# Pooling the queries two steps earlier, loading them one step earlier, and halving three long GpSimd operations

## The chip, the core and the metric

The kernel runs on one core of a Trainium2 chip. The metric is the device time of one execution in microseconds. The kernel before took 839.42 us (median of 3 runs, 837.78 to 840.08). The engines named below are TensorE (PE; its weight loads are PEld), VectorE (DVE), ScalarE (ACT), GpSimd (POOL), and SyncE (SP), which issues the DMA transfers.

## What is computed

The input is q, k and v of shape 4 x 8 x 1152 x 64 (batch, heads, sequence, width), in fp32. Neighbouring rows of q are averaged in twos, which leaves 576 queries per head; attention is taken over all 1152 keys; the heads are put side by side (512 columns), and a block follows with a layer norm, two weight matrices and a residual:

```python
q_pool = q.reshape(B, H, S // 2, 2, D).mean(axis=3)
scores = scale * np.matmul(q_pool, k.transpose(0, 1, 3, 2))
scores = scores - np.max(scores, axis=-1, keepdims=True)
attn = np.exp(scores)
attn = attn / (np.sum(attn, axis=-1, keepdims=True) + 1e-09)
x = np.matmul(attn, v)            # then heads side by side: 4 x 576 x 512
xn = (x - mu) / np.sqrt(var + 1e-06) * g_ln
out = x + np.maximum(xn @ w_ch1, 0.0) @ w_ch2     # w_ch1 512 x 2048, w_ch2 2048 x 512
```

## The kernel before, in words

**Pairs and steps.** Two heads of one batch are a pair; there are 16 pairs, p = 0 to 15. A pair's 1152 pooled query rows (576 of each head) are nine blocks of 128, and each block is a step, so there are 144 steps. Step i works on block i % 9 of pair i // 9. Its scores fill a slot of three banks of PSUM (128 x 1152, fp32); there are two slots, for even and odd steps. The function `step(i)` writes out by hand the order of work on every engine: the row maximum of step i on DVE (L384), its exponential on ACT (L398, into the tile `pe`, of which there are two), the scores of step i + 1 on PE (L365, L373), and further work for steps before and after.

**From the exponential to the product with v.** From step 36 on, the exponential is split into a high and a low fp16 part (tile `hl`). ACT makes the high part (L412). In the next step the low part is made: on DVE (L421), or, for the steps with i % 9 of 2, 5 or 8, on GpSimd as a scaling in place (L254, pe) and a subtraction (L419). Both read `pe`, so the exponential two steps later, which writes the same one of the two `pe` tiles, comes after them. SP then issues a transposing DMA of `hl` to `pt` (L424), and PE multiplies `pt` with v four steps after the scores (L467). Before step 36, transposes run on PE and this chain is absent.

**Queries.** `load_q(p)` (L122) loads the queries of pairs p and p + 1, p even, in four transfers of 288 KB, issued by SP; there are two such buffers. `pool_q(p)` (L161) adds neighbouring rows on GpSimd (one instruction, 128 x 1152). `bound(p, "q")` (L174) takes an upper bound of the sums on ACT (L188). `dup_q(p)` (L168) copies the sums beside themselves on GpSimd. `prep_q` then transposes and splits them (L328, L289, L286). For keys the same is done by `prep_k` (L300, L304).

**Where these are placed.** The list at L816 to L850 places each pair's preparation relative to i0 = 9(p - 1), the first step of the pair before it. `at(i, ...)` puts work at the end of step i, `pre(i, ...)` at its beginning. k is loaded at the end of step i0 - 1 and v at the end of i0. For p = 6, 8, 10, 12 and 14, the queries are loaded at the end of step i0 - 8, pooled at the beginning of step i0 - 5 (for p = 6, i0 - 6), bounded two steps after that, and copied at the end of step i0 - 1. For p = 2 and 4 another branch places them, in steps before 36.

**The block behind the attention.** From step 36 on, layer norm and the two matrix products run in between as "units": each step puts one unit on PE (L619 for the first matrix, L651 for the second), whose result goes from one of two PSUM banks through ACT (L632) and DVE (L633) at the beginning of the next step. ACT does these evacuations ahead of that step's exponential. The weights are loaded in steps 0 to 31 and scaled and split by GpSimd (`w_split_a`, `_b`, `_c`; the last is L797); those of the second half are split in steps 40 to 58. When all steps are over, PE alone works through the remaining units.

Every engine takes its instructions in the order in which they are written here, and an instruction that waits holds up all that are behind it on its engine.

Of the kernel before, what the change touches and what calls it, by code (L numbers as in the profile page):

```python
# [14 lines left out]
ALU = mybir.AluOpType  # L15
# [9 lines left out]
def tile_pooled_attention_moe(  # L25
# [18 lines left out]
    nc = tc.nc  # L44
# [4 lines left out]
    C = S // 128  # L49
# [30 lines left out]
    wsl = const.tile([128, 17, 2, 1024], FP16, name="wsl")  # L80
# [74 lines left out]
    def qt_of(p):  # L155
# [2 lines left out]
            st["qt"] = tr_p.tile([128, 2, 2 * C * 64], FP16, tag="qt", name="qt")  # L158
        return st["qt"]

    def pool_q(p, eng, halves=None):  # L161

        a = raws[p, "q"]
        for o, n in ((0, 128),) if halves is None else halves:
            x = a[o:o + n].rearrange("p h c r d -> p (h c) r d")
            eng.tensor_tensor(x[:, :, 0], x[:, :, 0], x[:, :, 1], op=ALU.add)

    def dup_q(p, eng, halves=None):  # L168
        a = raws[p, "q"]
        for o, n in ((0, 128),) if halves is None else halves:  # L170
            x = a[o:o + n].rearrange("p h c r d -> p (h c) r d")
            eng.tensor_copy(x[:, :, 1], x[:, :, 0])

    def bound(p, which, o=0, n=128, junk=None):  # L174
        st = state(p)
# [163 lines left out]
    def on_pe(i):  # L339

        return 0 <= i < HP * C
# [452 lines left out]

    def w_split_c(n):
        x = wsl[:, n + 1].rearrange("p a n -> p (a n)").bitcast(FP32)
        nc.gpsimd.tensor_tensor(wsl[:, n, 1], x, wsl[:, n, 0], op=ALU.subtract)  # L797
        w_done[n // 4] += 1


# [2 lines left out]
    def at(i, fn, *a):  # L803
        todo.setdefault(i, []).append((fn, a))
# [3 lines left out]
    def pre(i, fn, *a):  # L808
        early.setdefault(i, []).append((fn, a))
# [5 lines left out]
    for p in range(1, NP):  # L815
        i0 = (p - 1) * C  # L816
        at(max(i0 - 1, 0), load, p, "k", nc.sync)
        at(i0, load, p, "v", nc.sync)
        at(i0 + 1, bound, p, "k")
        if p % 2 == 0:  # L820
            if on_pe(i0):
                at(i0 - 4, load_q, p, (nc.sync,))
                at(i0 - 1, lambda p=p: calm.appendleft((lambda n: pool_q(p, nc.gpsimd), 0)))
                at(i0, lambda p=p: calm.appendleft((lambda n: dup_q(p, nc.gpsimd), 0)))
            else:
                x = i0 - (6 if p == 6 else 5)
                at(i0 - 8, load_q, p, (nc.sync,))
                pre(x, pool_q, p, nc.gpsimd)
                at(i0 - 1, dup_q, p, nc.gpsimd)
            at(i0 + 2 if on_pe(i0) else x + 2, bound, p, "q")  # L830
        elif p == 1:
            upper = (64, 64)
            pre(0, behind_scales)
            pre(i0 + 1, pool_q, 1, nc.gpsimd, (upper,))
            at(i0 + 1, dup_q, 1, nc.gpsimd, (upper,))
            at(i0 + 2, bound, 1, "q", *upper)
        else:
            at(i0 + 1, same_q, p)
        if not on_pe(p * C):
            at(i0 + 2, bound, p, "v")  # L840
        pre(i0 + 3, scales_reduce, p, 0, 2 if on_pe(p * C) else 3)
        for n in range(2):
            if on_pe(p * C):
                at(i0 + (5, 7)[n], gate)
            at(i0 + (5, 7)[n], take_v, p, n)
        for n, (fn, u) in enumerate(PREPS):
            late = 1 if on_pe(i0) else 0
            pre(i0 + 4 + n + late, lambda fn=fn, p=p, u=u: preps.append((fn, p, u)))

    for m in range(32):  # L850
        i0 = m
# [6 lines left out]
    this = [0]  # L858
# [3 lines left out]
    def w_splits(part):  # L862
        for n in range(4):
            if part < 2:
                calm.extend((fn, 4 * part + n) for fn in (w_split_a, w_split_b, w_split_c))
                continue
            i0 = 22 + 9 * part + 5 * n // 2
            for x, fn in ((0, w_split_a), (1, w_split_b), (2, w_split_c)):
                at(i0 + x, fn, 4 * part + n)
# [276 lines left out]
```

## Time and profile before

| | |
|---|---|
| median of 3 runs | 839.42 us (837.78 to 840.08) |
| the profiled execution | 839.62 us, its span 837.8 us |
| busy shares of the span | PE 97%, DVE 72%, ACT 67%, POOL 42% |
| mean granted TensorE clock | 0.993 |
| chain that ended last | PE 70%, DVE 12%, ACT 9%, DMA 4% |

A span is the time from the first instruction to the last; the profiled execution's own time is 1.8 us longer. A timeline row gives start and duration in us, the engine, the line of the kernel, the operation, what it writes and reads, its shape, how many instructions were merged, and in brackets the idle time of that engine before it with what ended it.

### The profile page before, as it was taken

To read this page: it belongs to the slowest core of one execution; us is meant where nothing else is said; L and a number is where in the kernel's file an instruction comes from. 1 tells how busy PE (TensorE), PEld (TensorE's weight loads), DVE (VectorE), ACT (ScalarE), POOL (GpSimd) and SP (SyncE) were. 2 spreads that over 40 slices of the span, in tenths; PEclk is the share of its full clock that TensorE was granted. 3 is DMA by queue.
4 is the path that set the end of the run, shared out by engine and by line. 5 is a ranking of instruction groups with operands and counts; after the bars stand their busy time and mean duration, and the time that the engine had idled before them with its cause. 6 is when DMAs were issued, how large, how long until landed. Compare 5 with 4: busy or idle time off the path is not lost.

```text
span 837.8 us, 21673 instructions
## 1 busy us (share of the span) xinstructions
PE 809.8 (97%) x9142; PEld 576.7 (69%) x9142; DVE 606.2 (72%) x1167; ACT 558.4 (67%) x810; POOL 351.8 (42%) x343
## 2 busy tenths in 40 slices
PE   7999999987999989999999999999999999999997
PEld 6787878776666666757576766766666767767764
DVE  3598989887888878797887878888787877522221
ACT  3999898976777868787776777677867676311110
POOL 3020334286899982456452553636343432200000
PEclk9999999999999999999999999999999999999999
DMA  6944474125698998899989988996969866401001
GB/s 146 256 164 156 141 210 163 43 60 113 115 181 141 194 172 191 153 185 185 167 147 166 212 167 144 176 196 113 204 125 194 137 126 131 95 2 26 14 1 25
DMA packets 276018, 115.97 MB, mean 138 GB/s; under 512 B 259280, under 2 KB 259280, under 8 KB 275920
## 3 DMA queue, kind: packets, MB, share of 16 engines
q1 hardware_dynamic: 275568, 113.70, 66.0%
q8 instruction: 71, 1.16, 0.6%
q10 hardware_dynamic: 352, 0.88, 0.5%
q14 instruction: 27, 0.22, 0.1%
HBM read 46.14 MB, written 4.72 MB: 61 GB/s over the span
## 4 chain that ended last, share of the span: by engine, by line
PE 70%; DVE 12%; ACT 9%; DMA 4%; issue 3%; POOL 1%; SPq 1%; ACTq 0%; DVEq 0%; POOLq 0%
PE psum L619 21%; PE psum L651 20%; PE psum L467 10%; PE psum L365 8%; ACT pe L398 3%; DVE mx L384 3%; PE psum L373 2%; PE psum L455 2%; DMA kr<-in_k_dram 2%; PE psum L328 2%; PE psum L431 1%; DVE hl L421 1%; ACT pt L437 1%; PE psum L300 1%; DMA stage<-in_moe_w_ch_dram 1%
## 5 line engine op out<-in xcount | busy, mean ns | idle before, releaser
L384 DVE TENSOR_REDUCE mx<-psum 128x1 f32<-128x1152 f32 x144 | 194.3, 1349 | 21.3 <-PE psum L204 6.9
L398 ACT ACTIVATE pe<-psum,nb,sc 128x1152 f32<-128x1152 f32 x144 | 188.6, 1310 | 13.8 <-DVE r L516 5.7
L651 PE MATMUL psum<-wsl,ht 128*128 128x512 f16 x864 | 196.7, 379 | 0.0
L619 PEld LDWEIGHTS <-wsl 128*128 128x128 f16 x1920 | 170.1, 98 | 22.8 <-issue 4.0
L619 PE MATMUL psum<-xn,wsl 128*128 128x256 f16 x1536 | 177.9, 274 | 3.6 <-DVE ht L633 2.8
L651 PEld LDWEIGHTS <-ht 128*128 128x128 f16 x864 | 80.5, 98 | 88.0
L632 ACT ACTIVATE ht<-psum 128x512 f16<-128x512 f32 x72 | 42.9, 596 | 135.4 <-PE psum L619 134.1
L365 PE MATMUL psum<-kt,qt 64*128 64x512 f16 (+1 forms) x960 | 127.4, 380 | 0.7 <-ACT pe L398 0.5
L412 ACT ACTIVATE hl<-pe 128x1152 f16<-128x1152 f32 x108 | 125.6, 1163 | 3.4
L467 PE MATMUL psum<-vt,pt 128*128 128x65 f16 (+1 forms) x3240 | 117.0, 193 | 0.3 <-DMA pt<-hl 0.3
L467 PEld LDWEIGHTS <-pt 128*128 128x128 f16 (+1 forms) x3240 | 108.5, 100 | 3.1 <-DMA pt<-hl 0.4
L421 DVE SCALAR_TENSOR_TENSOR hl<-pe,hl 128x1152 f16<-128x1152 f32 x72 | 109.4, 1519 | 0.0
L633 DVE SCALAR_TENSOR_TENSOR ht<-psum,ht 128x512 f16<-128x512 f32 x72 | 49.6, 689 | 71.6 <-ACT ht L632 71.6
L254 POOL TENSOR_SCALAR pe<-pe 128x1152 f32<-128x1152 f32 x36 | 42.4, 1178 | 140.5 <-ACT hl L412 140.5
L419 POOL TENSOR_TENSOR hl<-pe,hl 128x1152 f16<-128x1152 f32 x36 | 85.5, 2376 | 3.0
L455 PE MATMUL psum<-pt,vt 128*65 128x128 f32 (+1 forms) x720 | 78.9, 265 | 1.9 <-DVE qt L286 1.9
L455 PEld LDWEIGHTS psum<-pt,vt 128*65 128x65 f32 x720 | 73.1, 140 | 2.2 <-DVE qt L286 2.2
L365 PEld LDWEIGHTS <-qt 64*128 64x128 f16 (+1 forms) x960 | 39.6, 96 | 38.7 <-issue 22.1
L373 PEld LDWEIGHTS <-qt 128*128 128x128 f16 (+1 forms) x320 | 17.2, 99 | 62.9 <-issue 62.7
L286 DVE SCALAR_TENSOR_TENSOR qt<-psum,s,qt 128x384 f16<-128x384 f32 x48 | 29.5, 615 | 34.6 <-ACT qt L289 34.3
L260 POOL COPY gate<-gate 128x1 f32<-128x1 f32 x27 | 5.2, 194 | 110.9 <-DVE gate L259 110.9
L665 DVE SCALAR_TENSOR_TENSOR xb<-psum,inv,xb 128x512 f32<-128x512 f32 x32 | 23.8, 745 | 36.9 <-PE psum L651 36.9
(117 smaller groups left out, 1028.4 us busy)
## 6 DMA issues: line engine op xcount, KB each, us to landing
stage<-in_moe_w_ch_dram SPq DMA_DIRECT2D x32, 512.0 KB, 6.0
kr<-in_k_dram SPq DMA_DIRECT2D x16, 576.0 KB, 4.4
qr<-in_q_dram SPq DMA_DIRECT2D x31, 288.0 KB, 6.2
vr<-in_v_dram SPq DMA_DIRECT2D x15, 576.0 KB, 4.8
out_dram<-xb SPq DMA_DIRECT2D x32, 128.0 KB, 2.4
pt<-hl SPq DMA_TRANSPOSE x108, 4.7
kr<-in_k_dram SPq DMA_DIRECT2D x16, 64.0 KB, 4.1
vr<-in_v_dram ACTq DMA_DIRECT2D x1, 576.0 KB, 7.2
```

What stands on the lines that cost most here:

```text
L365: nc.tensor.matmul(out=sp[o:o + w, c0:c0 + 512], lhsT=qt[r:r + 64, qa, q0:q0 + w], rhs=kt[r:r + 64, ka, h], start=(a == 0), stop=(a == 2),)
L384: nc.vector.tensor_reduce(mx, st["s"], axis=AX.X, op=ALU.max)
L398: nc.scalar.activation(out=st["pe"], in_=st["s"], func=ACTF.Exp, scale=pair[i // C]["sc"][:, 0:1], bias=st["nb"],)
L412: nc.scalar.activation(out=hl[:, 0], in_=st["pe"], func=ACTF.Copy, scale=2.0 ** 15)
L419: nc.gpsimd.tensor_tensor(hl[:, 1], st["pe"], hl[:, 0], op=ALU.subtract)
L421: nc.vector.scalar_tensor_tensor(hl[:, 1], st["pe"], 2.0 ** 15, hl[:, 0], op0=ALU.mult, op1=ALU.subtract)
L455: nc.tensor.matmul(out=ps[0:65, q0:q0 + w], lhsT=vt[:, h, c], rhs=pt[:, 128 * u + q0:128 * u + q0 + w], start=(u == 0), stop=(u == C - 1),)
L467: nc.tensor.matmul(out=dst[:, 0:n], lhsT=lhsT, rhs=rhs, start=(u == 0 and lhsT is hi and n == 65), stop=(u == C - 1 and lhsT is lo), skip_ ...
L619: nc.tensor.matmul(out=ps[:, o:o + n], lhsT=wsl[:, 8 * w + cc, wa, f * 128:f * 128 + 128], rhs=xn[:, xa * KD + cc, 0:n], start=(m == 0), s ...
L632: lambda: nc.scalar.activation(out=hi, in_=pv, func=ACTF.Relu),
L633: lambda: nc.vector.scalar_tensor_tensor(lo, pv, 0.0, hi, op0=ALU.max, op1=ALU.subtract),
L651: nc.tensor.matmul(out=ps, lhsT=hv[0][:, ha, f, t * 128:t * 128 + 128], rhs=wsl[:, 8 * w + 4 + f // 2, wa, (f % 2) * DM:(f % 2) * DM + DM] ...
```

## The change

Three things change. In steps from 36 on, `pool_q`, `dup_q` and `w_split_c` issue two instructions, each for half of the columns, in place of one (`on_pe(i)` is true for steps 0 to 35; `this[0]` is the step being written). For p = 6, 8, 10, 12 and 14 the queries are loaded at the end of step i0 - 9 (was i0 - 8). For p = 8, 10, 12 and 14 they are pooled at the beginning of step i0 - 7 (was i0 - 5; p = 6 keeps i0 - 6), and for all five the bound follows one step after the pooling (was two).

```diff
+    def cuts(x):
+        return (x,) if on_pe(this[0]) else (x[:, 0:C], x[:, C:2 * C])
+
     def pool_q(p, eng, halves=None):
 
         a = raws[p, "q"]
         for o, n in ((0, 128),) if halves is None else halves:
             x = a[o:o + n].rearrange("p h c r d -> p (h c) r d")
-            eng.tensor_tensor(x[:, :, 0], x[:, :, 0], x[:, :, 1], op=ALU.add)
+            for y in cuts(x):
+                eng.tensor_tensor(y[:, :, 0], y[:, :, 0], y[:, :, 1], op=ALU.add)
 
     def dup_q(p, eng, halves=None):
...
-            eng.tensor_copy(x[:, :, 1], x[:, :, 0])
+            for y in cuts(x):
+                eng.tensor_copy(y[:, :, 1], y[:, :, 0])
...
     def w_split_c(n):
         x = wsl[:, n + 1].rearrange("p a n -> p (a n)").bitcast(FP32)
-        nc.gpsimd.tensor_tensor(wsl[:, n, 1], x, wsl[:, n, 0], op=ALU.subtract)
+        for y in (slice(0, 1024),) if on_pe(this[0]) else (slice(0, 512), slice(512, 1024)):
+            nc.gpsimd.tensor_tensor(wsl[:, n, 1, y], x[:, y], wsl[:, n, 0, y], op=ALU.subtract)
         w_done[n // 4] += 1
...
             else:
-                x = i0 - (6 if p == 6 else 5)
-                at(i0 - 8, load_q, p, (nc.sync,))
+                x = i0 - (6 if p == 6 else 7)
+                at(i0 - 9, load_q, p, (nc.sync,))
                 pre(x, pool_q, p, nc.gpsimd)
                 at(i0 - 1, dup_q, p, nc.gpsimd)
-            at(i0 + 2 if on_pe(i0) else x + 2, bound, p, "q")
+            at(i0 + 2 if on_pe(i0) else x + 1, bound, p, "q")
```

## Rows read from the trace of the kernel before

**Rows 1.** The page, part 1: busy us, share of the span, instructions.

```profile
PE 809.8 (97%) x9142; PEld 576.7 (69%) x9142; DVE 606.2 (72%) x1167; ACT 558.4 (67%) x810; POOL 351.8 (42%) x343
```

**Rows 2.** PE's waits from 215 to 730 us: total us, times, longest.

```profile
PE psum L619 <- DVE ht L633: 2.8, 2, 2.1
```

**Rows 3.** PE's timeline, one stretch for each of p = 8, 10, 12, 14.

```profile
303.74 4.34 PE L619 MATMUL psum<-xn,wsl 128*128 128x256 f16 x24 [2.14 <-DVE ht L633]
...
388.02 2.78 PE L619 MATMUL psum<-xn,wsl 128*128 128x256 f16 x24
...
477.59 2.75 PE L651 MATMUL psum<-wsl,ht 128*128 128x512 f16 x12
...
566.26 0.63 PE L574 MATMUL psum<-ident,xs 128*128 128x128 f32 x4 [1.77 <-DVE kt L286]
```

**Rows 4.** Windows: us, busy PE, PEld, DVE, ACT, POOL, granted PE clock, DMA share, GB/s.

```profile
303.70:308.10 4.40, 4.36 (x26) 3.23 (x25) 3.75 (x6) 2.43 (x3) 4.21 (x4) 0.63 0.69 132
```

**Rows 5.** DVE's timeline, the scales of pair 7.

```profile
298.79 1.84 DVE L240 TENSOR_SCALAR e<-red 128x3 int32<-128x3 int32 x1
```

**Rows 6.** SP's timeline: loads of v and q for p = 8, 10, 12.

```profile
285.01 0.58 SPq L119 DMA_DIRECT2D vr<-in_v_dram  x1
...
289.54 2.50 SPq L131 DMA_DIRECT2D qr<-in_q_dram  x4
...
370.84 0.58 SPq L119 DMA_DIRECT2D vr<-in_v_dram  x1
...
375.83 2.50 SPq L131 DMA_DIRECT2D qr<-in_q_dram  x4
...
457.88 0.58 SPq L119 DMA_DIRECT2D vr<-in_v_dram  x1
...
464.08 3.01 SPq L131 DMA_DIRECT2D qr<-in_q_dram  x4
```

**Rows 7.** GpSimd's timeline around the pooling for p = 8, 10, 12.

```profile
285.70 2.13 POOL L797 TENSOR_TENSOR wsl<-wsl 128x1024 f16<-128x1024 f32 x1
287.81 2.22 POOL L254 TENSOR_SCALAR wsl<-wsl,wscl 128x1024 f32<-128x1024 f32 x1
...
291.23 2.38 POOL L419 TENSOR_TENSOR hl<-pe,hl 128x1152 f16<-128x1152 f32 x1
...
297.98 2.62 POOL L166 TENSOR_TENSOR qr<-qr 128x1152 f32<-128x1152 f32 x1 [3.36 <-DMA qr<-in_q_dram]
...
375.92 1.16 POOL L254 TENSOR_SCALAR pe<-pe 128x1152 f32<-128x1152 f32 x1 [6.82 <-ACT hl L412]
...
384.58 2.62 POOL L166 TENSOR_TENSOR qr<-qr 128x1152 f32<-128x1152 f32 x1 [3.10 <-DMA qr<-in_q_dram]
...
473.31 2.62 POOL L166 TENSOR_TENSOR qr<-qr 128x1152 f32<-128x1152 f32 x1 [4.91 <-DMA qr<-in_q_dram]
```

**Rows 8.** ACT's timeline: exponentials of steps 40, 58, 76, 94, and two more.

```profile
210.89 1.31 ACT L398 ACTIVATE pe<-psum,nb,sc 128x1152 f32<-128x1152 f32 x1 [0.79 <-POOL hl L419]
...
289.44 1.16 ACT L188 ACTIVATE kt<-vr 128x1152 f16<-128x1152 f32 x1 [0.42 <-DMA vr<-in_v_dram]
...
295.08 1.31 ACT L398 ACTIVATE pe<-psum,nb,sc 128x1152 f32<-128x1152 f32 x1
...
380.75 1.31 ACT L398 ACTIVATE pe<-psum,nb,sc 128x1152 f32<-128x1152 f32 x1
...
383.48 0.69 ACT L289 ACTIVATE kt<-psum,s 128x512 f16<-128x512 f32 x1
...
471.23 1.31 ACT L398 ACTIVATE pe<-psum,nb,sc 128x1152 f32<-128x1152 f32 x1
```

**Rows 9.** The page, part 5: the evacuations of the first matrix's units.

```profile
L632 ACT ACTIVATE ht<-psum 128x512 f16<-128x512 f32 x72 | 42.9, 596 | 135.4 <-PE psum L619 134.1
...
L633 DVE SCALAR_TENSOR_TENSOR ht<-psum,ht 128x512 f16<-128x512 f32 x72 | 49.6, 689 | 71.6 <-ACT ht L632 71.6
```

**Rows 10.** The line of the copy of the sums: duration in ns, min/median/max.

```profile
L172 POOL COPY qr<-qr x9: 1142/1150/2323, 8.7 to 583.3; 128x1152 f32<-128x1152 f32 x7, 64x1152 f32<-64x1152 f32 x2
```

## The prediction

> **What bounds the kernel now.** I read the busy shares first, then who PE waited for, then the stretches around each pooling, engine by engine. The reader is to see that PE is busy for 97% of the span [rows 1]: what PE loses is lost for good, and what another engine loses costs nothing until PE waits for it. From 215 to 730 us, where the edits lie, PE waits little; the largest entry is 2.8 us in two waits of the first matrix's units (L619) for DVE [rows 2]. Of these, 2.14 us stand at 303.74, in the step of pair 7's scales [rows 3]. Their cause is on GpSimd. A DVE instruction on 128 x 3 numbers takes 1.84 us at 298.79 [rows 5], and ends just after GpSimd's pooling, which runs from 297.98 to 300.60 [rows 7]. After that wait the 24 matmuls take 4.34 us, where the same 24 take 2.78 at 388.02 [rows 3]: the granted clock is 0.63 in that stretch [rows 4], half speed for part of it. So an idle PE costs about 1.6 us more, at least where it stood for 2.1 us; at 566.26 a wait of 1.77 us was followed by no such slowing. These collisions are what the edits take away: 2.14 + 1.56 us at pair 8, and at most 1.77 at pair 14 [rows 3].
>
> **What moves on SP.** The four transfers of q go out one step sooner, directly behind the v transfer of the same step end: at 285.6 instead of 289.54 (285.01 + 0.58), at 371.4 instead of 375.83, at 458.5 instead of 464.08 [rows 6]. That is 3.9 to 5.6 us sooner. They also pass one transposing DMA, which now waits behind them (2.5 to 3.0 us of issuing). Its product with v comes four steps after the scores, and PE will be held by something later in the same steps (below), so I cost it at nothing; without that cover it would be up to 3 us a pair.
>
> **When the data is there.** Before, GpSimd stood 3.36, 3.10 and 4.91 us at the pooling until the data had landed, 8.44, 8.75 and 9.23 us after the first issue (297.98 - 289.54, and so on) [rows 6, 7]. That cost nothing: nothing urgent was behind it. Now v's 576 KB are directly ahead in the same queue; for pair 8 v landed 4.4 us after its issue (289.44 - 285.01) [rows 6, 8]. This adds between 0 and 4.4 us to q. I take 1.0, near the lower end, because v has landed 3.8 us after q's new issue, a time in which most of q was not there before either. The pooling can then begin at 285.6 + 9.4 = 295.0, 371.4 + 9.8 = 381.2 and 458.5 + 10.2 = 468.7.
>
> **What stands behind it.** The pooling moves two steps up GpSimd's queue and the data only one. It now stands in front of the low part of step i0 - 7 (56, 74, 92), which before ran at 290.0 to 293.6 (pair 8), and from 375.92 (pair 10) [rows 7]. GpSimd works in order, so this low part starts only after the data has landed and the pooling is done. Pooling: 2.62 us and 0.13 for a second instruction (bounds 0 and 0.19, for an instruction boundary; other extra instructions on GpSimd, some 20, come to 3 us over the whole run and lie in its idle time). Low part: 1.16 + 0.08 + 2.38 = 3.62. Pair 8 also has the halved split (2.13 + 0.13) and a scaling of weights (2.22, lower bound 1.1) in front [rows 7]. So the low parts end:
> pair 8: 295.0 + 2.75 + 2.26 + 2.22 + 3.62 = 305.9;
> pair 10: 381.2 + 2.75 + 3.62 = 387.5;
> pair 12: 468.7 + 6.37 = 475.1.
> The exponentials of steps 58, 76 and 94 write the same `pe` tile and began at 295.08, 380.75 and 471.23 [rows 8]. They become 10.8, 6.8 and 3.9 us late. That this wait is real is shown once already: at 210.89, where the pooling of pair 6 stands before step 38's low part in the same manner, ACT waited 0.79 us for GpSimd [rows 8]. The bound on ACT, one step earlier after the pooling, waits too (about 1.16 us of work, as at 289.44), but less long than the exponential behind it.
>
> **What PE loses.** Behind the late exponential come ACT's other work, then the evacuations that PE's next unit needs: 2.73 us from the exponential's start to the first evacuation (383.48 - 380.75) [rows 8], then 0.60 on ACT and 0.69 on DVE [rows 9], so 4.0 in all; at pair 10 a key block's 0.69 goes first, so 4.7. PE's unit moves
> at pair 8 from 303.74 to 305.9 + 4.0 = 309.9: +6.2;
> at pair 10 from 388.02 to 387.5 + 4.7 = 392.2: +4.2;
> at pair 12 from 477.59 to 475.1 + 4.0 = 479.1: +1.5 [rows 3].
> Pair 8's old wait and its slowing are inside the 303.74 and stay. Pair 14 lies as pair 12 does, but PE there already waits 1.77 us before 566.26; I put it between 0 and 1.5, at 0.7. Pair 10 would add one stretch at half clock, as at 303.74: +1.6. Pair 6 keeps its place and gets its data sooner; its 0.79 us go, but no wait of PE hangs on it in the rows: 0. Halves of `dup_q` and `w_split_c`: 0, beside work.
>
> Sum: 6.2 + 4.2 + 1.6 + 1.5 + 0.7 = +14.2. The profiled execution took 839.62, so 853.8; it lies 0.2 above the median of the runs, so 853.6 against 839.42.
>
> **A rule beside the rows.** GpSimd's copy of the sums takes 1.15 us in the median and 2.32 at most [rows 10]: GpSimd, too, is held up by something. The Trainium skill, SBUF — State Buffer, section "Who interferes with whom", says that a DVE instruction with two SBUF inputs and a reading GpSimd instruction exclude each other for a whole instruction, and that whichever came first keeps the other out. By that rule the second half of a pooling can lose its turn to DVE's low part, which speaks against halving: 1.17 us (2.32 - 1.15) in front of each of four late low parts, 4.7 us more in all, 858, which is inside the range below.
>
> **Rivals.** (A) The other side, faster: the data lands while GpSimd is idle, the pooling is over before its low part is due, and the collisions are gone. Gain: 2.14 + 1.56 + 1.77 = 5.5, so 834. It decides at pair 10: the pooling must be done by 375.92, so the data must be there by 373.2, 1.8 us after the issue. For it: GpSimd stood idle for 6.82 us before 375.92, just the room for a pooling [rows 7]. Against it: every load needed 8.4 us or more.
> The skill's rule from above stands behind this rival too: a DVE instruction shut out by a half waits half as long.
> (B) Only pair 8 pays, since PE's two score slots and its units swallow the 4 to 7 us at the others: 6.2, so 846. For it: ACT is busy for only 67% [rows 1]; against it: the first matrix's units wait for the evacuation of the same step.
> (C) Every pair pays the whole: v ahead costs the full 4.4 us, and each wait brings a slow clock. 3.4 x 4 + 1.6 x 2 = 17 more, so 871; with half of these 17 us, 862.
> (D) GpSimd's delay stays off PE's path: 839.6. Against it: the wait at 210.89.
>
> **How the numbers follow.** About 0.3% (2.5 us) is what can be told from no change. Chances: forecast 0.54 (its own range 847 to 860: without v's 1.0, the slow clock and half of the 2.22, it is 14.2 - 3.7 - 1.6 - 1.1 = 7.8, so 847; with two more microseconds of landing at three pairs, 860), A 0.11, B 0.17, C 0.12, D 0.06. Slower 0.54 + 0.17 + 0.12 = 0.83, same 0.06, faster 0.11. A range of 842 to 865 leaves out A, D and the uppermost part of C, 0.20 together.
>
> **What would show it.** GpSimd's two poolings for p = 10 start near 381, with a wait for DMA of 8 us or more ahead of them, and step 74's low part follows them, not before 384. ACT waits for GpSimd at the exponentials of steps 58, 76 and 94, which the rows of before show without a wait; PE shows gaps of 2 to 6 us there, some followed by a lower granted clock, and the scales of pair 7 run at 0.2 us each. The prediction is wrong if the poolings begin without a wait, or if PE has no gap after a late low part.

## The result and the profile after

The changed kernel takes 852.42 us (median of 4 runs, 850.33 to 854.45); the kernel before took 838.84 us beside it (4 runs, 837.78 to 840.08). The ratio is 1.015 [1.0121, 1.0179]: 13.6 us slower. The forecast was 853.6, in a range of 842 to 865. The profiled execution after is the slowest of the four, 854.45 us, span 852.6.

The first row below is the page's busy shares after, to hold against [rows 1].

```profile
PE 815.6 (96%) x9142; PEld 580.3 (68%) x9142; DVE 604.8 (71%) x1167; ACT 558.1 (65%) x810; POOL 358.2 (42%) x363
```

The span grew by 14.8 us. PE stood idle for 837.8 - 809.8 = 28.0 us before and 852.6 - 815.6 = 37.0 after: 9.0 of the 14.8. The other 5.8 are PE being busy longer on the same 9142 instructions. What it waited for, from 215 to 745 us (total, times, longest), to hold against [rows 2]:

```profile
PE psum L472 <- DMA pt<-hl: 8.9, 4, 4.3
PE psum L579 <- DVE kt L291: 4.3, 2, 2.4
...
PE psum L624 <- DVE ht L638: 0.9, 2, 0.6
```

The first entry was next to nothing before (L467, 0.3 us in one wait): the product with v (L472, L467 before) waits for the transposing DMA. `kt` had one wait before, of 1.77 us [rows 3]. The timeline of PE shows where:

```profile
301.07 1.65 PE L472 MATMUL psum<-vt,pt 128*128 128x65 f16 x27 [4.28 <-DMA pt<-hl]
...
303.18 4.82 PE L624 MATMUL psum<-xn,wsl 128*128 128x256 f16 x24
...
310.87 2.78 PE L624 MATMUL psum<-xn,wsl 128*128 128x256 f16 x24
...
390.69 0.99 PE L472 MATMUL psum<-vt,pt 128*128 128x65 f16 x27 [3.19 <-DMA pt<-hl]
...
397.03 0.63 PE L579 MATMUL psum<-ident,xs 128*128 128x128 f32 x4 [1.83 <-DVE kt L291]
...
483.05 0.99 PE L472 MATMUL psum<-vt,pt 128*128 128x65 f16 x27 [0.89 <-DMA pt<-hl]
...
572.30 0.99 PE L472 MATMUL psum<-vt,pt 128*128 128x65 f16 x27 [0.53 <-DMA pt<-hl]
...
579.75 0.63 PE L579 MATMUL psum<-ident,xs 128*128 128x128 f32 x4 [2.44 <-DVE kt L291]
```

Each of the four moved poolings has its wait for `pt`; the two with a wait of 3 us or more are pairs 8 and 10. At pairs 10 and 14 a second wait follows, for a key block (`kt`) that DVE evacuates late. After the 4.28 us the next 24 matmuls take 4.82 us, and not the 2.78 they take at full clock [rows 3]. They are the unit that ran at 296.58 before, though. The unit that waited 2.14 us for `ht` at 303.74 [rows 3] is now the one at 310.87: 7.1 us later, without a wait, and at full clock.

The result of each unit is evacuated by ACT and DVE; DVE's part, for these two units of pair 8:

```profile
300.68 0.69 DVE L638 SCALAR_TENSOR_TENSOR ht<-psum,ht 128x512 f16<-128x512 f32 x1 [4.41 <-ACT ht L637]
...
310.12 0.69 DVE L638 SCALAR_TENSOR_TENSOR ht<-psum,ht 128x512 f16<-128x512 f32 x1 [1.85 <-ACT ht L637]
```

They end at 301.37 and 310.81. ACT's part of the first stands behind the bound of 298.90, that of the second behind the exponential of 306.89 (both below). The first is 0.3 us behind the landing of `pt`, the second 0.06 us ahead of its unit: at pair 8 the late evacuations come at the same time as the late DMA.

Where the transposing DMA stands is on SP's queue. After, in two places:

```profile
286.58 0.58 SPq L119 DMA_DIRECT2D vr<-in_v_dram  x1
287.20 2.41 SPq L131 DMA_DIRECT2D qr<-in_q_dram  x4
...
376.95 0.58 SPq L119 DMA_DIRECT2D vr<-in_v_dram  x1
377.57 2.44 SPq L131 DMA_DIRECT2D qr<-in_q_dram  x4
380.18 7.00 SPq L429 DMA_TRANSPOSE pt<-hl  x1
```

and before, the one that stood between v and q:

```profile
371.58 4.20 SPq L424 DMA_TRANSPOSE pt<-hl  x1
```

Before, this transposing DMA was issued 0.7 us after v and took 4.20 us to issue. After, it is issued 3.2 us after v (380.18 - 376.95), has four transfers of q ahead of it as well, and takes 7.00 us. From its issue to its landing it took 6.3 us before and 10.5 after; at pair 8 5.9 before (285.75) and 11.2 after.

GpSimd after, the poolings (two halves, L170) and the low parts (L424) behind them, for p = 8, 10 and 14, to hold against [rows 7]:

```profile
296.12 2.75 POOL L170 TENSOR_TENSOR qr<-qr 128x576 f32<-128x576 f32 x2 [9.68 <-DMA qr<-in_q_dram]
...
304.49 2.37 POOL L424 TENSOR_TENSOR hl<-pe,hl 128x1152 f16<-128x1152 f32 x1
...
386.45 2.75 POOL L170 TENSOR_TENSOR qr<-qr 128x576 f32<-128x576 f32 x2 [11.75 <-DMA qr<-in_q_dram]
...
390.40 2.38 POOL L424 TENSOR_TENSOR hl<-pe,hl 128x1152 f16<-128x1152 f32 x1
...
568.15 1.41 POOL L170 TENSOR_TENSOR qr<-qr 128x576 f32<-128x576 f32 x1 [11.74 <-DMA qr<-in_q_dram]
570.52 1.40 POOL L170 TENSOR_TENSOR qr<-qr 128x576 f32<-128x576 f32 x1 [0.97 <-DVE r L522]
```

ACT after, the bounds (L193) and the exponentials (L403) of steps 58 and 76, to hold against [rows 8]:

```profile
298.90 1.16 ACT L193 ACTIVATE qr<-qr 128x1152 f32<-128x1152 f32 x1 [3.03 <-POOL qr L170]
...
306.89 1.31 ACT L403 ACTIVATE pe<-psum,nb,sc 128x1152 f32<-128x1152 f32 x1 [6.25 <-POOL hl L424]
...
389.23 1.16 ACT L193 ACTIVATE qr<-qr 128x1152 f32<-128x1152 f32 x1 [3.14 <-POOL qr L170]
...
392.81 1.31 ACT L403 ACTIVATE pe<-psum,nb,sc 128x1152 f32<-128x1152 f32 x1 [1.84 <-POOL hl L424]
```

The exponential of step 58 starts 0.03 us after its low part has ended (304.49 + 2.37 = 306.86), that of 76 likewise. These waits were forecast, and they are there.

The longer busy time of PE is its clock. Three stretches, after (us; busy us of PE, PEld, DVE, ACT, POOL with instructions; granted PE clock; DMA share; GB/s):

```profile
186.00:206.00 20.00, 15.81 (x115) 11.88 (x114) 13.61 (x25) 12.80 (x17) 17.25 (x18) 0.83 0.70 138
296.00:312.00 16.00, 11.13 (x111) 8.26 (x108) 9.56 (x16) 6.78 (x10) 15.53 (x14) 0.79 0.80 116
574.00:590.00 16.00, 13.28 (x150) 8.74 (x149) 11.64 (x24) 10.40 (x14) 9.29 (x14) 0.89 0.69 133
```

the same stretches before:

```profile
186.00:206.00 20.00, 14.84 (x122) 10.99 (x123) 13.98 (x29) 13.81 (x19) 13.41 (x13) 0.91 0.62 139
296.00:312.00 16.00, 13.86 (x147) 9.83 (x144) 14.30 (x23) 9.46 (x14) 13.47 (x10) 0.89 0.87 159
574.00:590.00 16.00, 16.00 (x210) 11.64 (x209) 12.89 (x20) 12.18 (x18) 13.67 (x10) 1.00 0.70 123
```

Time lost at half speed is the stretch times what its clock lacks to 1.00: (0.17 - 0.09) x 20 = 1.6 us more than before in the first, 0.10 x 16 = 1.6 in the second, 0.11 x 16 = 1.8 in the third, 5.0 together, most of the 5.8. The second stretch has the wait of 4.28 us, the third that of 2.44. The first lies ahead of the four moved poolings; the run with the pooling behind the low part (below), whose order is the same up to step 56, was granted 1.00 there, so I count it as scatter of this one execution, which is 2.0 us above its median. That leaves 3.4 us beside the waits of this change. And a wait does not always bring a slow clock: at pair 10, with waits of 3.19 and 1.83 us, the clock was full,

```profile
380.00:404.00 24.00, 17.41 (x233) 13.27 (x232) 17.44 (x35) 15.81 (x23) 10.94 (x14) 1.00 0.97 189
```

### The profile page after: what moved, and what is told of

The parts are those of the page before. It is cut to its first block, busy times and chain, and to the rows that moved or that the text cites. A ratio compares the mean times of both kernels' runs of the same rounds, so it can differ in the third digit from the quotient of the medians.

```text
span 852.6 us, 21686 instructions
## 1 busy us (share of the span) xinstructions
PE 815.6 (96%) x9142; PEld 580.3 (68%) x9142; DVE 604.8 (71%) x1167; ACT 558.1 (65%) x810; POOL 358.2 (42%) x363
## 4 chain that ended last, share of the span: by engine, by line
PE 62%; POOL 11%; DVE 9%; ACT 9%; DMA 4%; issue 3%; SPq 1%; POOLq 0%; ACTq 0%; DVEq 0%
PE psum L656 19%; PE psum L624 17%; PE psum L472 9%; PE psum L370 7%; ACT pe L403 3%; DVE mx L389 3%; PE psum L460 3%; POOL wsl L259 3%; POOL hl L424 3%; PE psum L378 2%; POOL wsl L803 2%; DMA qr<-in_q_dram 2%; PE psum L436 2%; PE psum L333 1%; POOL pe L259 1%
## 5 line engine op out<-in xcount | busy, mean ns | idle before, releaser
L403 ACT ACTIVATE pe<-psum,nb,sc 128x1152 f32<-128x1152 f32 x144 | 188.5, 1309 | 25.9 <-POOL hl L424 14.9
L472 PE MATMUL psum<-vt,pt 128*128 128x65 f16 (+1 forms) x3240 | 118.4, 194 | 8.9 <-DMA pt<-hl 8.9
L472 PEld LDWEIGHTS <-pt 128*128 128x128 f16 (+1 forms) x3240 | 109.8, 101 | 12.2 <-DMA pt<-hl 9.6
L424 POOL TENSOR_TENSOR hl<-pe,hl 128x1152 f16<-128x1152 f32 x36 | 85.5, 2374 | 3.0
```

The costliest lines, as they stand in the source:

```text
L403: nc.scalar.activation(out=st["pe"], in_=st["s"], func=ACTF.Exp, scale=pair[i // C]["sc"][:, 0:1], bias=st["nb"],)
L424: nc.gpsimd.tensor_tensor(hl[:, 1], st["pe"], hl[:, 0], op=ALU.subtract)
L472: nc.tensor.matmul(out=dst[:, 0:n], lhsT=lhsT, rhs=rhs, start=(u == 0 and lhsT is hi and n == 65), stop=(u == C - 1 and lhsT is lo), skip_ ...
```

## The experiments

Two theories were set against each other. **W**, that of the prediction: GpSimd stands at the pooling until q has landed, the low part behind it is late, and with it the exponential. **Q**: the transfers of q, issued directly behind v, hold up the transposing DMA behind both, and PE waits for `pt`. The table gives, for the profiled executions, the start of the row maximum at some steps, less that of the kernel before; a jump between two columns is what the pooling in between costs (p = 6 before 54, then p = 8, 10, 12, 14). The first column is scatter of the start. The jump for p = 6 lies between -1.3 and +3.1 among the versions with a sooner load, and is not read here.

| kernel | 36 | 54 | 72 | 90 | 108 | 126 | end | median us | ratio |
|---|---|---|---|---|---|---|---|---|---|
| changed kernel | -0.8 | +0.7 | +5.6 | +10.5 | +11.7 | +14.8 | +14.8 | 852.42 | 1.015 [1.0121, 1.0179] |
| loads alone | +1.1 | +4.2 | +6.3 | +12.5 | +13.1 | +11.6 | +11.6 | 850.53 | 1.0129 [1.0099, 1.0159] |
| poolings alone | +0.9 | +2.3 | +12.9 | +22.2 | +29.1 | +34.4 | +34.4 | 869.54 | 1.0366 [1.0326, 1.0407] |
| halves alone | -1.5 | -0.9 | -3.3 | -1.8 | -1.9 | -3.0 | -3.0 | 836.39 | 0.9967 [0.9951, 0.9983] |
| both moves, no halves | -1.2 | +1.0 | +6.5 | +11.2 | +12.8 | +15.4 | +15.4 | 856.23 | 1.0203 [1.0161, 1.0244] |
| load two steps sooner still | -1.2 | +0.4 | +0.4 | +2.6 | +2.6 | +0.4 | +0.4 | 839.56 | 1.0015 [1.0000, 1.0030] |
| pooling behind the low part | -2.0 | -3.3 | -1.1 | +3.3 | +4.2 | +2.9 | +2.9 | 845.43 | 1.0101 [1.0072, 1.0129] |
| pooling late, halves | -1.9 | -1.6 | -4.1 | -3.2 | -3.2 | -4.2 | -4.2 | 835.92 | 0.9973 [0.9958, 0.9987] |
| half of q sooner | -1.9 | +1.2 | +0.8 | +2.0 | +2.0 | +3.5 | +3.5 | 839.56 | 1.0014 [0.9997, 1.0032] |
| poolings alone, bound later | -0.9 | -0.9 | +6.5 | +13.6 | +20.5 | +28.4 | +28.4 | 870.02 | 1.0393 [1.0346, 1.0439] |
| changed kernel, bound later | -0.1 | -0.7 | +5.5 | +11.6 | +16.5 | +22.3 | +22.3 | 857.23 | 1.0237 [1.0199, 1.0275] |

The kernel before took 838.84 us beside the changed kernel, 839.36 beside the next four rows (loads, poolings, halves, both moves), 838.24 beside the four after them and 837.66 beside the last two. A difference between rows with different neighbours is therefore uncertain by about 1 us.

**Loads alone.** Kernel before, with

```diff
-                at(i0 - 8, load_q, p, (nc.sync,))
+                at(i0 - 9, load_q, p, (nc.sync,))
```

> The kernel before with one edit: the queries are loaded at the end of step i0 - 9 instead of i0 - 8. Theory W (the loss comes from GpSimd, which stands at the pooling and holds the low part behind it): the pooling keeps its late place, its data comes a step sooner, so nothing is lost: 837 to 839 us. Rival Q (the loss comes from the queue: q directly behind v delays the transposing DMA behind both, and the product with v waits for it): the product waits for pt as in the changed kernel, where these waits sum to 8.9 us at four places, so 846 to 850 us, with the pooling itself on time.

850.53 us, 11.2 slower, with the poolings where they always were. PE's waits:

```profile
PE psum L467 <- DMA pt<-hl: 8.0, 4, 3.6
```

As many waits, at the same line, as in the changed kernel, and hardly any other; GpSimd waited 1.0 us for q in all. So Q is real, and alone it costs nearly as much as the whole change (11.2 of the 16.9 us that both moves cost with whole operations, below).

**Poolings alone.** Kernel before, with

```diff
-                x = i0 - (6 if p == 6 else 5)
+                x = i0 - (6 if p == 6 else 7)
...
-            at(i0 + 2 if on_pe(i0) else x + 2, bound, p, "q")
+            at(i0 + 2 if on_pe(i0) else x + 1, bound, p, "q")
```

> The kernel before with one edit: the queries are pooled at i0 - 7 (bound one step behind), the load stays at i0 - 8. Theory W: the data now lands some 4 us later than in the changed kernel while the low part waits behind it, so the exponentials are 4 us later still at each of four pairs: 860 to 872 us, slower than the changed kernel. Rival Q: v and q are a step apart again, so the products with v do not wait: 838 to 843 us.

869.54 us, 30.2 slower. PE does not wait for `pt`; it waits for what comes behind a late ACT, among the entries:

```profile
PE psum L619 <- DVE ht L633: 12.4, 3, 7.3
PE psum L300 <- DVE ht L633: 8.3, 2, 5.1
PE psum L365 <- ACT pe L398: 7.3, 3, 5.6
```

and GpSimd stood up to 20.1 us at a pooling:

```profile
POOL qr L166 <- DMA qr<-in_q_dram: 71.3, 5, 20.1
```

So W is real too. GpSimd stands longer here than in the changed kernel (71.3 us at its poolings, against 47.8 at the four moved ones there), since the data comes a step later; so 30 is not W's price in the changed kernel. Each theory is enough by itself for a slower kernel. Their prices, 11 and 30, don't add: in the changed kernel the late evacuations and the late DMA reach PE in the same microseconds (pair 8 above), and each hides part of the other.

**Halves alone.** Kernel before, with `cuts` and the three split operations of the change, and nothing moved.

> The kernel before with the halved instructions alone. If DVE waits for whole GpSimd instructions, as the 1.84 us on 128 x 3 numbers suggests, the wait of PE at the scales of pair 7 (2.1 us and a slow clock behind it) shrinks by about half and the clock need not fall: 836 to 838 us. If the halves only add instruction boundaries, or lose their turn to DVE: 839 to 841 us.

836.39 us: 0.33% faster, 3.0 us, clear of 1. At pair 8 PE shows why:

```profile
301.77 2.78 PE L624 MATMUL psum<-xn,wsl 128*128 128x256 f16 x24 [0.25 <-DVE ht L638]
```

Here it waited 2.14 us before, and the same 24 matmuls took 4.34 [rows 3]: 1.89 + 1.56 = 3.45 us gone. DVE's instruction in front of it is shorter:

```profile
298.28 1.11 DVE L245 TENSOR_SCALAR e<-red 128x3 int32<-128x3 int32 x1
```

where it was 1.84 [rows 5]. It now ends at 299.39, when the first half of the pooling that began at 297.96 (two halves in 2.75) is over.

**Both moves, no halves.** The changed kernel without `cuts`.

> The changed kernel without the halves (both moves, whole instructions). Theories W and Q both say that the moves make the loss, so 851 to 855 us, like the changed kernel's 852.4. If the halves have a part in it by losing their turn to DVE, this one is faster by up to 4 us: 848.

856.23 us, 3.8 above the changed kernel's 852.42; the intervals of the two ratios overlap, so this alone shows no difference, but the sign is that of the run before. So the two moves cost some 17 us, and the halves give some 3 back.

**Load two steps sooner still.** Changed kernel, with

```diff
-                at(i0 - 9, load_q, p, (nc.sync,))
+                at(i0 - (9 if p == 6 else 11), load_q, p, (nc.sync,))
```

> The changed kernel with one edit: for p = 8 to 14 the queries are loaded two steps sooner still (end of step i0 - 11), away from v's load and three steps before the pooling at i0 - 7. W and Q (each alone is enough for most of the loss) both go: GpSimd finds its data, and no transposing DMA stands behind v and q together. 833 to 838 us, as the halves alone or somewhat faster. If pooling at i0 - 7 costs by itself (GpSimd's time in front of the low part, DVE shut out): 840 to 845.

839.56 us. Both waits are gone, from GpSimd's poolings (but for 1.66 us at p = 12) and from PE's product with v, and 12 to 13 us with them. It missed both of its ranges. One reason in the rows is that k is now late. k's issue before:

```profile
365.24 0.57 SPq L115 DMA_DIRECT2D kr<-in_k_dram  x1
```

and SP, ACT and PE in this run:

```profile
364.02 4.44 SPq L429 DMA_TRANSPOSE pt<-hl  x1
368.56 0.52 SPq L115 DMA_DIRECT2D kr<-in_k_dram  x1
...
373.74 1.16 ACT L193 ACTIVATE kt<-kr 128x1152 f16<-128x1152 f32 x1 [1.58 <-DMA kr<-in_k_dram]
...
376.73 0.84 PE L370 MATMUL psum<-kt,qt 64*64 64x512 f16 x12 [2.15 <-ACT pe L403]
```

On SP q's four transfers (from 360.03), two output transfers and a transposing DMA stand ahead of k. It goes out 3.3 us later than before, of which 0.4 is this run's own lag (column 72), and is there 5.2 us after its issue, 4.3 before. ACT's bound on it stands in front of the exponential, and PE waits 2.15 us for that; at pair 8 it is 1.52. So what is delayed behind q need not be the transposing DMA. But not everything behind q pays: the one at 364.02 comes much closer behind q than k, landed 8.1 us after its issue, and PE did not wait for it. In the kernel before, too, one stands behind q (379.77, 7.4 us to landing) without a wait.

**Pooling behind the low part.** Changed kernel, the load as there, for p of 8 and more

```diff
-                pre(x, pool_q, p, nc.gpsimd)
+                (pre if p == 6 else at)(x + (0 if p == 6 else 1), pool_q, p, nc.gpsimd)
...
-            at(i0 + 2 if on_pe(i0) else x + 1, bound, p, "q")
+            at(i0 + 2 if on_pe(i0) else x + (1 if p == 6 else 2), bound, p, "q")
```

> The changed kernel with one edit: for p = 8 to 14 the pooling is issued behind the low part of step i0 - 7 (end of step i0 - 6, bound one step later), so that GpSimd's wait for the data holds up no low part. The load stays directly behind v. If W has its share in the changed kernel's loss beside Q: 846 to 849 us, the load alone (850.5) less the halves' 3. If Q covers W fully: 852. If W were the whole of it: 836.

845.43 us: 7.0 under the changed kernel (6.4 with each against the kernel before beside it; four runs, 842.55 to 849.45), and a little under the 846 to 849 of the theory that W has its share. The waits for `pt` stay, those for `kt` (L579) are gone:

```profile
PE psum L472 <- DMA pt<-hl: 7.7, 4, 3.5
```

So W's share on top of Q is 6 to 7 us. What is left, 845.43 against halves alone at 836.39, is Q: 9.0, or 10.2 with each against the kernel before beside it. That is close to the 11.2 of the load alone.

**Pooling late, halves.** Changed kernel with the load back at i0 - 8 and, for p of 8 and more, the pooling at i0 - 4.

> A kernel meant to beat both: the halves, the load where it was (i0 - 8; p = 6 as well), and for p = 8 to 14 the pooling one step later than before (i0 - 4), behind the scales of the pair before, bound one step behind it. If the collision of the pooling with the scales of step i0 - 5 is what the halves leave over: 834 to 836 us, against 836.4 for the halves alone. If the pooling there delays taking v and the low part of step i0 - 4: 838 to 842.

835.92 us, 0.27% faster than before and no different from halves alone. PE's largest entry here is 1.7 us, and its wait for `pt` is

```profile
PE psum L472 <- DMA pt<-hl: 0.5, 2, 0.3
```

This and halves alone are the two versions that beat both kernels.

**Half of q sooner.** Kernel before, two of the four transfers at i0 - 9, directly behind v, and two where all were:

```diff
-                at(i0 - 8, load_q, p, (nc.sync,))
+                at(i0 - 9, load_q, p, (nc.sync,), (0,))
+                at(i0 - 8, load_q, p, (nc.sync,), (1,))
```

> The kernel before with the load in two parts: pair p's half of q at the end of step i0 - 9, directly behind v, pair p + 1's half at the end of i0 - 8. Pooling where it was. Theory Q as a matter of bytes ahead of the transposing DMA: with 576 KB instead of 1152 KB behind v, the transposing DMA lands some 4 us sooner than with the whole load, and the product with v waits little: 838 to 842 us. If it is the place directly behind v whatever the bytes: 847 to 851, as the whole load one step sooner (850.5).

839.56 us, no change that can be told, and

```profile
PE psum L467 <- DMA pt<-hl: 2.1, 2, 1.1
```

against 8.0 with all four ahead. The wait hangs on how much is queued in front of the transposing DMA. The one behind v and half of q (374.39) landed 9.1 us after its issue, between the 6.3 behind v alone and the 10.5 behind v and all of q. Fewer bytes and fewer transfers to issue go together here; the run does not part them.

**Which part of W.** ACT has two instructions that wait for a late GpSimd: the bound, for the pooling, and the exponential, for the low part. In two more kernels the bound of pairs 8 to 14 comes one step later, in poolings alone and in the changed kernel:

```diff
-            at(i0 + 2 if on_pe(i0) else x + 1, bound, p, "q")
+            at(i0 + 2 if on_pe(i0) else x + (1 if p == 6 else 2), bound, p, "q")
```

> The kernel before with the poolings of pairs 8 to 14 two steps earlier, their bound on ACT two steps after the pooling (one step in the pooling-only run, 869.5 us), the loads where they were. If the late low part and its exponential hold PE (my prediction's chain), the bound does not matter: 866 to 872 us, ACT's waits for GpSimd's low part at 15 us or more. If it is the bound, which stands on ACT ahead of the evacuations of the same step and waits for the pooling, most goes: 845 to 858, and the wait of 7.3 us of the first matrix's units for DVE's evacuation is gone or below 3 us.

> The changed kernel with the bound of pairs 8 to 14 two steps after the pooling (was one). If the late exponential is what is left of GpSimd's hold beside the transposing DMA: 850 to 854 us, as the changed kernel (852.4), with PE's waits of 1.8 and 2.4 us for the key blocks still there. If the bound carries it: 844 to 848, as the kernel with the pooling behind the low part (845.4). In both, PE's waits for pt stay at 7.5 to 9 us, since the loads are where they were.

The first took 870.02 us (1.0393 [1.0346, 1.0439]), as poolings alone took 869.54: the bound is not what holds PE. The wait for `ht` is down to 2.9 us in all, as the other theory wanted, but others took its place:

```profile
PE psum L574 <- DVE kt L286: 8.3, 1, 8.3
PE psum L365 <- ACT pe L398: 7.5, 3, 4.8
PE psum L574 <- POOL xs L568: 7.0, 1, 7.0
```

The last is a carrier that the prediction did not have: the layer norm's scaling (`xs`) stands on GpSimd behind the same low part. The second kernel took 857.23 us (1.0237 [1.0199, 1.0275]), slower than the changed kernel and outside both expectations. Its waits for `pt` are 8.6 us; the key blocks' grew from 4.3 to

```profile
PE psum L579 <- DVE kt L291: 7.3, 2, 5.0
```

In its rows the bound now runs between the late exponential and the key block's evacuation, 1.15 us in front of it; that this alone makes the 4.8 us is argued, not shown.

## Why the prediction was right, and where it was not

**The total** came out within 1.2 us, and the mechanism it rested on is there. The closeness is in part luck. By pairs the terms were +6.2, +5.8, +1.5 and +0.7, and the table has +4.9, +4.9, +1.2 and +3.1: three too large, one too small. The path to them has one failed step, and several terms were mis-sized.

**Data and low parts: right.** The poolings were put at 295.0, 381.2 and 468.7; they began at 296.12, 386.45 and 478.61. The second is 380.8 and the third 468.1 on the clock of before, since by then the kernel ran 5.6 and 10.5 late (columns 72 and 90). Waits for DMA of 9.68, 11.75, 14.64 and 11.74 us stand ahead of the four. The low parts were to end at 305.9, 387.5 and 475.1: they ended at 306.86 and, less 5.6 and 10.5, at 387.2 and 474.4. The exponentials of steps 58, 76 and 94 wait for GpSimd. The 1.0 us for v ahead of q was 0.1 to 0.5: q was there 8.9, 8.9 and 9.5 us after its first issue (296.12 - 287.20, and so on), against 8.4, 8.8 and 9.2 before.

**From the exponential to PE, at pair 8: right.** The unit of 303.74 was forecast for 309.9; it began at 310.87, and its evacuation ended at 310.81, 3.9 us behind the start of the late exponential (forecast 4.0). The term is smaller than forecast because the old slow clock did not stay: the unit takes 2.78 us and not 4.34. With the 0.7 of column 54, 7.1 - 0.7 - 1.56 = 4.9.

**The failed step: "so I cost it at nothing".** That was the transposing DMA which q's transfers pass on SP, with "without that cover it would be up to 3 us a pair" beside it. The cover was to be the late evacuation behind the exponential. But the product with v stands ahead of the unit, and at all four pairs PE met the DMA first: 8.9 us in all, 4.28 at pair 8, against 4.3 in waits for `kt`, which answer to W. The cover was not wrong altogether: at pair 8 the late evacuations were there no sooner than the DMA, so either cause would by itself have held PE about as long. That is read from the rows; no run has W alone with the data as soon as in the changed kernel. What the runs show is that a kernel that cures only W keeps half of the loss (845.43), that Q alone costs 11.2 us, and that with both cured 1.3 of the 13.6 is left (839.56). The bound of 3 us a pair was too low as well, because it counted only the time to issue q, 2.5 to 3.0. The transposing DMA itself took longer too: 7.00 us to issue behind v and q, 4.20 behind v alone, and 10.5 to landing against 6.3. The Trainium skill, DMA: Bandwidth & Descriptors, section "Queues, rings and completion order", says that a DMA engine takes the descriptors of one ring in order, and that SP owns one ring on each; the runs agree: 8.0 us of waits with all of q ahead, 2.1 with half of it.

**Pair 10: the slow clock (+1.6) did not come.** The clock was 1.00 there (window above). The 4.9 us are the waits of 3.19 and 1.83.

**Halves: 0 was wrong by 3 us.** The prediction named the collision (2.14 us and 1.56 of clock at pair 8) and then let it stay inside the new schedule. Halves alone gave 3.0, and with whole operations the changed kernel took 3.8 us more. Part of the reasoning held: DVE is still caught at pair 7's scales in the changed kernel, not by a pooling but by the low part that has moved there,

```profile
305.02 1.87 DVE L245 TENSOR_SCALAR e<-red 128x3 int32<-128x3 int32 x1
```

which ends at 306.89, as GpSimd's row of 304.49 ends at 306.86. So "the scales of pair 7 at 0.2 us each" failed. The opposite worry, that a second half loses its turn to DVE, shows once in the four poolings, 0.97 us at 570.52, which the profile puts down to DVE's small instructions and not to its low part; I had priced it at 1.17 for each. In the Trainium skill's rule (SBUF — State Buffer, "Who interferes with whom") the loser waits for the end of the winner's instruction; the 1.84 that became 1.11 when the instruction was cut agrees.

**Pair 14: +0.7 was too little.** It cost 3.1: its wait of 1.77 us for a key block [rows 3] became 2.44, the new one for `pt` adds 0.53, and now a stretch at half clock follows (granted 0.89 in the window above, 1.8 us), which after the 1.77 did not.

**Rivals.** A needed q within 1.8 us of its issue; it was there after 8.9. B (846) and C (862 to 871) are outside the measured interval, though C's picture, that every pooling pays fully, is close to poolings alone.

**What stays open.** How the 13.6 us divide between W and Q has no single answer: taking W away gives 6 to 7, and what then remains above halves alone is 9 to 10. When a slow clock follows a wait of PE is open too: it followed waits of 2.14 (before), 2.44 and 4.28 us, and not those of 1.77 (before) and 3.19, so the length of the wait alone does not decide it.

## What to carry to other kernels

When a load is issued earlier, look at what is urgent behind it in its own queue, and count as its delay the time to issue the load and the time in which its data moves ahead: here the transposing DMA was issued 2.5 us later behind v and took 4.2 us more to land. The same transfers cost 11 us directly behind v, nothing that can be told when cut in two, and little (1.3 us, with k late instead) two steps sooner still. When an instruction that waits for a transfer moves up an in-order engine by more steps than the transfer does, everything between its old and new place inherits the wait; putting it behind the next urgent instruction gave back half of the loss. A long GpSimd operation beside small DVE ones is worth cutting even where GpSimd is idle half of the time: that was the only gain here.

## What was not expected of the hardware

- A transposing DMA behind plain loads takes longer to issue, not only to land: 7.00 us behind v and q, 4.20 behind v alone, 2.70 at 362.49 of the kernel before, where no load stands just ahead. SP's next DMA is late by it as well: the output transfer behind all of them goes out 10.3 us after v (387.28 - 376.95), 7.6 before (378.43 - 370.84).
- A half of a pooling that takes 1.40 us alone came later beside DVE's low part: in the run with the load two steps sooner, where that low part ran from 370.13 to 372.03, the two halves lasted

```profile
369.40 3.89 POOL L170 TENSOR_TENSOR qr<-qr 128x576 f32<-128x576 f32 x2
```

where they take 2.75 at 296.12, that is 1.1 us more: close to the 1.17 that the prediction put on a second half that loses its turn.
- PE's clock made a fifth to a third of the profiled loss (3.4 us, or 5.0 with the stretch counted as scatter, of 14.8): each of the stretches from 296 and 574 us lost 1.6 to 1.8 us more than before, beside idle times of 4.28 and 2.44 us, and the one with 3.19 us lost none.
